# Attention, routed MoE and gated MLP on one core: a second expert item taken before all tokens are routed

## Chip, cores, metric
One NeuronCore of a Trainium2 chip runs the kernel. The metric is device time of one execution in microseconds (us), the median of the runs shown. All inputs come from the reference's own setup with seed 0.

## The reference, cut to what matters
```python
# attention: B=8, H=8, S=576, D=64; k and v are averaged over 8 neighbours (72 keys)
k_p = k.reshape(B, H, 72, 8, D).mean(axis=3); v_p = v.reshape(B, H, 72, 8, D).mean(axis=3)
attn = softmax(q @ k_p^T / sqrt(D)); x = (attn @ v_p) as (4608, 512)

# mixture of experts: 8 experts, one for each token; 512 -> 1024 -> 512
e_idx = argmax(x @ w_gate, axis=1)
gate_w = softmax(x @ w_gate)[e_idx]; eom = sigmoid(x @ w_output_gate)
for e in range(8):
    mask = e_idx == e
    out[mask] = gate_w[mask] * eom[mask, e] * (relu(x[mask] @ w1[e]) @ w2[e])

# gated MLP: 512 -> 2048 -> 512
h = out @ w_in; y = (h * sigmoid(h)) @ w_out
```

## The kernel before
The order of the instructions on every engine is written out by hand (`tc.manual_schedule()`): each engine works off its own queue in the order in which the Python code emits, and waits at an instruction whose operands aren't there.

**Attention.** The 4608 tokens are 36 tiles of 128. The loop over `u` (L790) runs two half-steps for each tile, u = 2 to 74; step u turns probabilities (`turn_p`, tile `psp`), multiplies by the values (`values`, tile `pv`, three steps late) and computes scores two or three steps ahead. After a tile's values follow its normalised rows (`r`, `xg` on VectorE), written to the DRAM table `xd`, and its gate logits (`gh`, `gl`).

**Routing.** Tiles are routed in groups (`GROUPS`). When the last tile of a group is in, `gate_ops` gives 21 small operations: the token's expert, its place in the expert's list by the `rank` matmuls, its weight. They go to a background queue from which `bg` takes 2 or 4 a step. Then each tile of the group is scattered by one GpSimd indirect DMA (`scatter`, L585, with six small memsets ahead of it, L584) into the table `idd`: one slot of (token, weight) for each token, sorted by expert. `SCAT` says how many steps after the group's end the scatters start, and how many go in two steps.

**The early item.** After group `EARLY` (24 tiles) `early_ops` picks the expert with most tokens so far. GpSimd gathers the ids and weights of its first 3 x 128 tokens from `idd` (`e_gid`, L652, in step `EG`), TensorE turns them (`e_ps`, L661, in step `ET`), and GpSimd gathers the tokens' rows from `xd` (`e_x`, L636, in step `EX`). These three blocks are the first item of the next stage, which can so begin before all tokens are routed.

**Expert items.** The MoE stage is a row of items, each with three, two or one block of 128 tokens of one expert (A, C and S in `ORDER`). Item 0 is the early one. An item of two or three blocks has 8 units; unit u is `l2(u)` (9 matmuls `y`, L1219, for three blocks) behind `l1(u+1)` (12 matmuls `h`, L1173). Weights come as four pairs of 512 KB loads on SyncE's queue (`load_w`, L1096 and L1099), after SyncE has read the expert's number (L1092), and are split into high and low parts on ScalarE and VectorE. Rows of an item are gathered by `gather_x` (L1121), turned by `trans_x` (`trx`, L1143) and split. Items of at most the fixed numbers of `ORDER` run always; what the counted tokens need beyond them runs behind a branch.

**What `pre` puts into item 0.** The dict `pre` holds what follows `l2(u)` of a unit: the last group's gate operations in -1 and 0, then its four scatters; the eight scatters of the group before (`kept_scat`) at the stage's start; the plan of the other items (`route`, 28 small VectorE operations) in units 1 and 2; the gather of all items' ids (`gather_ids`, tile `gid`, L891); in unit `GSTEP` = 5 `turn_ids`, which turns the ids on TensorE (`psi`, L1047) into `idx`, and the gather of item 1's rows. From unit 6 on the MLP's weights are decoded beside the items.

Finished items are scattered to the DRAM table `yd` (the early one is written to `ye`), from which the MLP stage reads its blocks (`yin`).

Of the kernel before, what the change touches and what calls it, by code (L numbers as in the profile page):

```python
# [8 lines left out]
F32 = mybir.dt.float32  # L9
# [19 lines left out]
GROUPS = (8, 12, 4, 8, 4)  # L29
# [10 lines left out]
SLOTS = ((NBLK - 3 + E - 1) // 3, 2 * E, E)  # L40
EARLY = 3
PACE = 6
REST = N - 3 * P
# [5 lines left out]
GSTEP = 5  # L49
# [36 lines left out]
STARTV = ((26, 2), (44, 3))  # L86
ORDER = "ACACASACACASACA"
# [31 lines left out]
def kernel(  # L119
# [30 lines left out]
    ye = tc.dram_tile([3 * P, DM], F32, name="ye")  # L150
# [479 lines left out]
    e_idx = const.tile([P, 1], I32, tag="e_idx", name="e_idx")  # L630
    e_ids = const.tile([P, 3], I32, tag="e_ids", name="e_ids")
    e_w = const.tile([P, 3], F32, tag="e_w", name="e_w")
    e_x = [lp.tile([P, DM], F32, tag=f"e_x{i}", name=f"e_x{i}") for i in range(3)]

    def early_x(i):
        nc.gpsimd.indirect_dma_start(  # L636
            out=e_x[i],
            out_offset=None,
            in_=xd[0 : G0[EARLY] * P, :],
            in_offset=bass.IndirectOffsetOnAxis(ap=e_ids[:, i : i + 1], axis=0),  # L640
        )

    def early_ops():
        def tl(shape, tag, dt=F32):
            return lp.tile(shape, dt, tag=f"e_{tag}", name=f"e_{tag}")

        n = tl([P, E], "n")
        mx, cand, best, row = tl([P, 1], "mx"), tl([P, E], "cand"), tl([P, 1], "best"), tl([P, 1], "row", I32)
        gid, gif = tl([3, P, 2], "gid", I32), tl([3, P], "gif")
# [9 lines left out]
        def turn():  # L659
            ps = bank("e_ps", "pr")  # L660
# [23 lines left out]
            lambda: nc.vector.tensor_tensor(out=row, in0=cand[:, 0:1], in1=pcol, op=ALU.add),  # L684
            lambda: nc.vector.scalar_tensor_tensor(
                out=e_off, in0=e_hot, scalar=-3.0 * P, in1=ebase, op0=ALU.mult, op1=ALU.subtract
            ),
        ], gather, lambda: nc.vector.tensor_copy(out=gif, in_=gid[:, :, 0]), turn
# [102 lines left out]
    kept_scat = []  # L791
    UN = 2 * NT
    for u in range(2, UN + PVL):
# [22 lines left out]
        if odd and 0 <= t < NT:  # L816
            gates(t)
            if t + 1 in G0:
                g = G0.index(t + 1) - 1
                ops, scat = gate_ops(g, gp if g < NG - 2 else lp, rank_ps)  # L820
                (at(GAT[g], bgq.extend, ops) if g in GAT else bgq.extend(ops))
                for i, f in enumerate(scat):
                    step = u + SCAT[g][0] + 2 * i // SCAT[g][1]
                    if step < UN + PVL:
                        at(step, f)
                    else:
                        kept_scat.append(f)
                if g + 1 == EARLY:
                    ops, ga, tu, tv = early_ops()
                    bgq.extend(ops)  # L830
                    at(EG, ga)
                    at(ET, tu)
                    item.append((ET, tv))
                    for i in range(3):
                        at(EX, early_x, i)
# [805 lines left out]
```

## Time and profile before
| | us |
|---|---|
| median of 3 runs | 1490.28 |
| the runs | 1485.74, 1490.87, 1490.28 |
| the profiled execution | 1488.13 |
| its span in the trace | 1486.4 |

| engine | busy, us | share of the span |
|---|---|---|
| TensorE (PE) | 1422.4 | 96% |
| VectorE (DVE) | 934.0 | 63% |
| ScalarE (ACT) | 652.5 | 44% |
| GpSimd (POOL) | 395.5 | 27% |

A busy share is the time in which an engine had an instruction in work. The profile also gives the clock that TensorE was granted in a stretch, as a fraction of 2.4 GHz: 1.00 is the upper of its two levels, 0.50 the lower (1.2 GHz). The span mean is 0.987. A timeline row gives the start of an instruction (or of several merged ones), its length, engine, line, operation, the tile written <- the tiles read, and in brackets the engine's idle time before it with what ended that. Attention runs to about 197 us, the expert items to about 700 us, the MLP to the end.

### The profile page before, as it was taken

Reading aid. Unit: us, or ns where it says so; the run is one execution under the profiler, and the core shown is the slowest. Engines: PE = TensorE matmul, PEld = TensorE weight load, DVE = VectorE, ACT = ScalarE, POOL = GpSimd, SP = SyncE. Lnnn points to the kernel's source line nnn. Section 1 sums busy time; section 2 is a strip of 40 time slices with the busy share of each in tenths; the row PEclk is TensorE's granted clock in tenths of the full one; section 3 lists DMA queues with packets and bytes.
Section 4 is the critical chain, followed back from the end, with each engine's and each line's share of the span. In section 5 each row is a group of like instructions: output and inputs, shape, how many; then the busy total and the mean of one; then the engine's idle time right before and its main releaser. Section 6 shows DMA issues by size and latency. Waiting matters only on the chain.

```text
span 1486.4 us, 22198 instructions
## 1 busy us (share of the span) xinstructions
PE 1422.4 (96%) x7923; PEld 1262.0 (85%) x7924; DVE 934.0 (63%) x1709; ACT 652.5 (44%) x1312; POOL 395.5 (27%) x629
## 2 busy tenths in 40 slices
PE   8999895999999999999999999999999999999996
PEld 6989784898989988898888888888888988988885
DVE  5677682889879778874753555645555565465443
ACT  4767542555566555662332423433343243234222
POOL 1766662446445334531020200120030012001001
PEclk9999997999999999999999999999999999999998
DMA  9999166688787766884989566567458557645441
GB/s 263 264 228 193 54 171 179 205 284 286 253 306 280 251 218 234 302 232 124 336 276 284 177 162 186 162 180 184 147 178 172 182 159 194 179 139 191 159 135 43
DMA packets 259370, 302.88 MB, mean 204 GB/s; under 512 B 157849, under 2 KB 190620, under 8 KB 250419
## 3 DMA queue, kind: packets, MB, share of 16 engines
q1 hardware_dynamic: 247042, 271.06, 62.4%
q0 software_dynamic: 11776, 29.53, 5.5%
q8 instruction: 64, 1.05, 0.3%
q10 hardware_dynamic: 432, 0.79, 0.1%
q14 instruction: 56, 0.45, 0.1%
HBM read 251.70 MB, written 50.41 MB: 203 GB/s over the span
## 4 chain that ended last, share of the span: by engine, by line
PE 41%; DVE 4%; ACT 4%; another core or an unknown queue 1%; issue 1%; DMA 1%; SPq 1%; POOL 0%; ACTq 0%; POOLq 0%; DVEq 0%
PE o L1455 22%; PE b L1411 8%; PE a L1411 6%; DVE sg L1429 1%; ACT gh L1432 1%; ACT t L1009 1%; SPq L985 1%; ACT os L1465 1%; DMA wQ<-wid 1%; DVE gl L1437 1%; DVE b L1010 0%; ACT sg L1425 0%; DVE t L1010 0%; DMA yin<-yd 0%
## 5 line engine op out<-in xcount | busy, mean ns | idle before, releaser
L1455 PE MATMUL o<-woh,gh 128*128 128x512 f32 x576 | 228.2, 396 | 1.3 <-ACT gh L1432 1.1
L1455 PE MATMUL o<-wol,gh 128*128 128x512 f32 x576 | 228.8, 397 | 0.0
L1455 PE MATMUL o<-woh,gl 128*128 128x512 f32 x576 | 228.0, 396 | 0.0
L1467 POOL DMA_INDIRECT out_dram<-os,ids x33 | 35.7, 1083 | 623.3 <-ACT os L1465 619.4
L1432 ACT CAST gh<-sg 128x384 fp32r<-128x384 f32 x192 | 98.6, 513 | 146.3 <-DVE sg L1429 145.1
L1437 DVE TENSOR_TENSOR gl<-sg,gh 128x384 fp32r<-128x384 f32 x192 | 107.3, 559 | 75.4 <-ACT gh L1432 64.6
L1455 PEld LDWEIGHTS o<-woh,gl 128*128 128x128 f32 x576 | 108.1, 188 | 28.9 <-DVE gl L1437 3.4
L1455 PEld LDWEIGHTS o<-woh,gh 128*128 128x128 f32 x576 | 108.1, 188 | 22.2 <-ACT gh L1432 4.5
L1455 PEld LDWEIGHTS o<-wol,gh 128*128 128x128 f32 x576 | 108.1, 188 | 17.3
L1425 ACT ACTIVATE sg<-a 128x384 f32<-128x384 f32 x56 | 27.5, 491 | 165.5 <-PE a L1411 157.9
L1411 PE MATMUL a<-b,wA 128*128 128x384 f32 x480 | 98.0, 339 | 2.0 <-ACT t L1572 2.0
L1411 PE MATMUL b<-t,wS 128*128 128x384 f32 x480 | 97.2, 336 | 0.2
L1411 PEld LDWEIGHTS a<-b,wA 128*128 128x128 f32 x480 | 85.6, 188 | 6.9 <-ACT t L1572 3.3
L1411 PEld LDWEIGHTS b<-t,wS 128*128 128x128 f32 x480 | 85.2, 188 | 5.6 <-DVE u L1420 1.8
L503 PE MATMUL pv<-vb,pT 72*128 72x128 f32 (+1 forms) x640 | 80.7, 277 | 0.3 <-DVE gh L537 0.3
L1420 DVE TENSOR_TENSOR u<-b,t 128x384 f32<-128x384 f32 x40 | 22.3, 557 | 89.1 <-PE b L1411 86.5
L503 PEld LDWEIGHTS pv<-vb,pT 72*128 72x128 f32 (+1 forms) x640 | 73.6, 182 | 2.0 <-issue 1.2
L482 ACT ACTIVATE pe<-sc,nm 128x72 f32<-128x72 f32 x288 | 67.7, 319 | 11.9 <-DVE nm L476 11.6
L1425 ACT ACTIVATE sg<-t 128x384 f32<-128x384 f32 x40 | 21.0, 525 | 108.9 <-DVE t L1420 102.7
L1429 DVE TENSOR_TENSOR sg<-a,sg 128x384 f32<-128x384 f32 x56 | 31.1, 555 | 48.6 <-ACT sg L1425 45.3
L492 ACT COPY pT<-psp 72x512 f32<-72x512 f32 x72 | 41.8, 581 | 40.3 <-PE psp L488 36.3
L476 DVE TENSOR_REDUCE nm<-sc 128x4 f32<-128x288 f32 x72 | 32.4, 452 | 29.9 <-PE sc L466 19.0
(3780 smaller groups left out, 3589.0 us busy)
## 6 DMA issues: line engine op xcount, KB each, us to landing
wS<-wis SPq DMA_DIRECT2D x40, 1024.0 KB
wA<-wid SPq DMA_DIRECT2D x40, 768.0 KB
wol<-wold SPq DMA_DIRECT2D x112, 256.0 KB
wQ<-wid SPq DMA_DIRECT2D x16, 1024.0 KB
yin<-yd SPq DMA_DIRECT2D x44, 192.0 KB
xd<-xg SPq DMA_DIRECT2D x32, 256.0 KB
raw_i<-in_moe_w_in_dram SPq DMA_DIRECT2D x16, 512.0 KB
wid<-em SPq DMA_DIRECT2D x8, 1024.0 KB
```

Source lines behind the costliest of these rows:

```text
L476: nc.vector.tensor_reduce(out=nm_t[u], in_=sc_t[u], op=ALU.max, axis=AX.X, negate=True)
L482: nc.scalar.activation(out=pe[:, h * NK : h * NK + NK], in_=ps[:, h, :], func=AF.Exp, bias=nm[:, h, :])
L492: nc.scalar.copy(out=pT_t[u], in_=ps_t.pop(u))
L503: nc.tensor.matmul(pv_t[t][o : o + n, j % 2, VW * c : VW * c + VW], pT[:, j, o : o + n], vw[b][:, HG * h : HG * h + VW], start=True, stop= ...
L1411: nc.tensor.matmul(ps, w[:, o, i, c, :], x[:, c, :], start=(first and k == 0), stop=(k == 5), skip_group_check=True)
L1420: nc.vector.tensor_tensor(out=o, in0=a, in1=b, op=ALU.add)
L1425: nc.scalar.activation(out=g_t[key][0], in_=h, func=AF.Sigmoid)
L1429: nc.vector.tensor_tensor(out=sg, in0=h, in1=sg, op=ALU.mult)
L1432: nc.scalar.copy(out=gh, in_=sg)
L1437: nc.vector.tensor_tensor(out=gl, in0=sg, in1=gh.bitcast(F32), op=ALU.subtract)
L1455: nc.tensor.matmul(o_t[sb, a][s], x[:, sl_], w, start=(k0 == 0 and k == 0), stop=(k0 == 2 * NFP - 1 and k == 2))
L1467: ins = nc.gpsimd.indirect_dma_start(out=out, out_offset=bass.IndirectOffsetOnAxis(ap=(id_t[b][:, s, 0:1] if b else e_ids[:, s : s + 1]), ...
```

## The change
A second early item is taken after 28 tiles, besides the one after 24. `early_ops(k)` runs twice; the second pick takes the expert with most tokens left (the first pick's 384 are off its count) and, if it is the same expert, the next three blocks (`both`). Item 1 is now that second early item: its ids are turned by a second `e_ps` behind unit 0, and its rows gathered right there through `e_ids[1]`. The first planned item is item 2, whose rows follow `turn_ids` in unit `GSTEP` = 9 where item 1's followed in unit 5. `ORDER` loses one A; the other 14 items stay in their order, so there are 16 items and 39 blocks before and after. The groups are 12, 8, 4, 4, 8 tiles; all of the first four are scattered within attention (`kept_scat` is gone), and the last group, now 8 tiles, has its gate operations and its scatters in units 1 and 2. `ye` holds six blocks and `yd` three fewer.

```diff
-GROUPS = (8, 12, 4, 8, 4)
+GROUPS = (12, 8, 4, 4, 8)
-SLOTS = ((NBLK - 3 + E - 1) // 3, 2 * E, E)
-EARLY = 3
+EARLY = (3, 4)
+NE = len(EARLY)
+SLOTS = ((NBLK - 3 * NE + E - 1) // 3, 2 * E, E)
-GSTEP = 5
+GSTEP = 9
-EG = 63
-ET = 66
-EX = 68
-GAT = {0: 27}
-SCAT = ((13, 2), (11, 3), (9, 2), (10, 2))
+EG = (61, 72)
+ET = 69
+EX = 71
+SCAT = ((12, 2), (6, 3), (6, 4), (6, 4))
-STARTV = ((26, 2), (44, 3))
-ORDER = "ACACASACACASACA"
+STARTV = ((26, 2), (40, 3))
+ORDER = "CACASACACASACA"
...
+        else:
+            ops += [
+                lambda: nc.vector.tensor_tensor(out=n, in0=hot, in1=e_hot, op=ALU.mult),
+                lambda: nc.vector.tensor_reduce(out=both, in_=n, op=ALU.add, axis=AX.X),
+                lambda: nc.vector.tensor_tensor(out=best, in0=cand[:, 0:1], in1=pcol, op=ALU.add),
+                lambda: nc.vector.scalar_tensor_tensor(
+                    out=row, in0=both, scalar=3.0, in1=best, op0=ALU.mult, op1=ALU.add
+                ),
...
-        bg(4 if u >= 52 or GAT[0] <= u < GAT[0] + 6 else 2)
+        bg(4 if u >= 44 or 28 <= u < 34 else 2)
...
             def rows(j, i):
+                if items[j][1] < 0:
+                    return e_ids[-1 - items[j][1]][:, i : i + 1]
                 c = col(j, i)
...
-                    src = e_idx[0:1, :] if items[j][1] < 0 else eji[p : p + 1, :]
+                    src = e_idx[-1 - items[j][1]][0:1, :] if items[j][1] < 0 else eji[p : p + 1, :]
...
-                    nc.scalar.dma_start(out=ye[i * P : (i + 1) * P, :], in_=ys)
+                    nc.scalar.dma_start(out=ye[j * TB + i * P : j * TB + (i + 1) * P, :], in_=ys)
...
-                if fc == (7 if pre and j == 0 else 3 if one else GU):
+                if not early and fc == (3 if one else GU):
...
+        def turn_late():
+            turn_e[0]()
+            turn_e[1](pby.tile([P, 512], F32, tag="y", name="e_ps"))()
+
         pre = {
-            -2: kept_scat,
-            -1: gate[:turn],
-            0: gate[turn + 1 :] + scat,
-            1: route[:14],
-            2: route[14:] + [gather_ids],
-            GSTEP: [turn_ids, "gather"],
+            0: [turn_late, 1],
+            1: gate[:turn],
+            2: gate[turn + 1 :] + scat,
+            4: route[:14],
+            5: route[14:],
+            6: [gather_ids],
+            GSTEP: [turn_ids, 2],
...
-            pre[7 + i // 3] = ranks[i : i + 3]
-        pre[13] = [turn_ranks]
+            pre[10 + i // 3] = ranks[i : i + 3]
+        pre[14] = [turn_ranks]
```

TensorE at the end of unit 5, before (`y` is l2, `h` is l1; `psi` turns the gathered ids, `xt` are item 1's rows):

```order
L1219 MATMUL y_0_-1_0_3274<-hi_0_-1_2_3379,hl_-1_5_3489 128x512
L1047 MATMUL psi<-ident,rkf 128x79
L1048 MATMUL psi<-ident,gid 128x79
L1143 MATMUL trx_-1_1_3545<-ident,xt_0_-1_1_3537 128x128 x4
L1173 MATMUL h_-1_7_3560<-xh_-1_0_3194,hi_0_-1_3_3424 128x384
```

TensorE at the end of unit 9, the second unit of item 1, in the changed kernel:

```order
L1243 MATMUL y_0_-1_1_3709<-hi_0_-1_4_3577,hh_-1_9_3694 128x512
L1243 MATMUL y_0_-1_1_3709<-lo_0_-1_4_3578,hh_-1_9_3694 128x512
L1243 MATMUL y_0_-1_1_3709<-hi_0_-1_4_3577,hl_-1_9_3695 128x512
L1069 MATMUL psi<-ident,rkf 128x76
L1070 MATMUL psi<-ident,gid 128x76
L1197 MATMUL h_-1_11_3788<-xh_-1_1_3568,hi_0_-1_5_3635 128x384
```

The two turns of the gathered ids stood behind 6 units of matmuls and right ahead of a turn of the rows fetched by them; now they stand behind 10 units, and two units of matmuls follow before the first rows fetched by them are turned.

TensorE near the end of attention, before (`e_ps` turns the ids of the early item):

```order
L466 MATMUL sc_1_2785<-kbd_116,qT_2659 128x144 x2
L661 MATMUL e_ps<-ident,e_gif 128x3
L662 MATMUL e_ps<-ident,e_gid 128x3
L488 MATMUL psp_2797<-ident,pe_2740 72x128 x4
L503 MATMUL pv_2811<-vb_1879,pT_2711 128x128 x4
L466 MATMUL sc_0_2816<-kbd_116,qT_2728 128x144 x2
```

The same place in the changed kernel, followed to the first turn of item 0's rows:

```order
L489 MATMUL psp_2936<-ident,pe_2884 72x128 x4
L504 MATMUL pv_2950<-vb_1706,pT_2835 128x128 x4
L667 MATMUL e_ps<-ident,e_gif_2646 128x3
L668 MATMUL e_ps<-ident,e_gid_2645 128x3
L489 MATMUL psp_2965<-ident,pe_2915 72x128 x4
L504 MATMUL pv_2950<-vb_1706,pT_2882 128x128 x4
L489 MATMUL psp_2983<-ident,pe_2945 72x128 x4
L504 MATMUL pv_2990<-vb_1706,pT_2913 128x128 x4
L504 MATMUL pv_2990<-vb_1706,pT_2943 128x128 x4
```

The turn has moved three steps towards the end: two `psp` steps and their values now stand behind it, where there were five.

GpSimd from the scatters of the last group to the gathers of the first planned items, before (`sli_4` are that group's slots, `xt` item 1's rows, `e_x` item 2's):

```order
L585 DMA idd<-idw,sli_4_3110 37888x2
L891 DMA gid<-idd,rowi 79x256
L1121 DMA xt_0_-1_1_3537<-xd,idx 128x512
L1121 DMA xt_0_-1_1_3539<-xd,idx 128x512
L1121 DMA xt_0_-1_1_3541<-xd,idx 128x512
L1121 DMA e_x_152<-xd,idx 128x512
L1121 DMA e_x_153<-xd,idx 128x512
```

GpSimd in the changed kernel, from the same scatters (`mh_i` and `em` belong to the decode of the MLP's weights, `e_x` are item 2's rows):

```order
L586 DMA idd<-idw,sli_4_3156 37888x2
L913 DMA gid<-idd,rowi 76x256
L252 TENSOR_TENSOR mh_i_0_3665<-mh_i_0_3665,em_0_3670 128x512
L272 TENSOR_TENSOR em_0_3670<-mh_i_0_3665,e_i_0_3623 128x4x128
L1145 DMA e_x_155<-xd,idx 128x512
L1145 DMA e_x_156<-xd,idx 128x512
```

Item 1's three gathers no longer stand behind `gid`, and a pair of decode operations stands between `gid` and item 2's gathers.

## Rows read from the trace of the kernel before

**Rows 1.** The page: busy time of each engine, and TensorE in 40 slices.

```profile
PE 1422.4 (96%) x7923; PEld 1262.0 (85%) x7924; DVE 934.0 (63%) x1709; ACT 652.5 (44%) x1312; POOL 395.5 (27%) x629
PE   8999895999999999999999999999999999999996
```

**Rows 2.** Stretches: length, busy of PE, PEld, DVE, ACT, POOL, clock, DMA share, GB/s.

```profile
180.00:186.00 6.00, 2.04 (x11) 1.93 (x12) 2.21 (x10) 1.53 (x6) 2.71 (x9) 0.61 0.01 2
240.00:250.00 10.00, 1.43 (x7) 1.22 (x8) 0.47 (x2) 0.22 (x1) 3.52 (x4) 0.50 0.26 74
270.00:300.00 30.00, 28.10 (x150) 24.52 (x149) 26.29 (x44) 14.80 (x23) 13.75 (x10) 1.00 0.75 245
```

**Rows 3.** Timeline of PE, end of attention.

```profile
169.03 0.60 PE L488 MATMUL psp<-ident,pe 128*72 128x128 f32 x4
...
170.85 0.60 PE L488 MATMUL psp<-ident,pe 128*72 128x128 f32 x4
...
183.96 0.26 PE L661 MATMUL e_ps<-ident,e_gif 3*128 3x3 f32 x1 [5.86 <-DVE e_gif L688]
...
184.26 1.07 PE L488 MATMUL psp<-ident,pe 128*72 128x128 f32 x4
...
187.79 0.76 PE L488 MATMUL psp<-ident,pe 128*72 128x128 f32 x4
...
196.89 0.60 PE L1143 MATMUL trx_-1_0_3196<-ident,e_x 128*128 128x128 f32 x4
...
201.88 0.66 PE L1173 MATMUL h_-1_0_3226<-xh_-1_0_3194,hi_-1_0_3190 128*128 128x384 f32 x1 [3.52 <-issue]
```

**Rows 4.** Timeline of POOL, end of attention and item 0.

```profile
175.16 0.97 POOL L585 DMA_INDIRECT idd<-idw,sli  x1 [0.16 <-issue]
...
177.10 0.96 POOL L585 DMA_INDIRECT idd<-idw,sli  x1 [0.16 <-issue]
181.47 0.92 POOL L652 DMA_INDIRECT e_gid<-idd,e_row  x1 [3.41 <-issue]
...
188.31 0.95 POOL L636 DMA_INDIRECT e_x<-xd,e_ids  x1 [0.30 <-issue]
...
233.82 1.93 POOL L891 DMA_INDIRECT gid<-idd,rowi  x1 [9.07 <-DMA r_-1_5_3472<-in_moe_w_dram]
245.56 0.99 POOL L1121 DMA_INDIRECT xt_-1_1_3537<-xd,idx  x1 [9.81 <-DVE idx L1049]
```

**Rows 5.** Timeline of DVE, end of attention and item 0.

```profile
196.66 0.16 DVE L617 TENSOR_SCALAR e<-ex 128x8 f32<-128x8 f32 x1
...
201.70 0.68 DVE L1146 TENSOR_TENSOR xl_-1_0_3195<-trx_-1_0_3210,xh_-1_0_3194 128x512 fp32r<-128x512 f32 x1
...
211.96 0.18 DVE L623 RECIPROCAL idw<-sm 128x4 f32<-128x4 f32 x1
...
244.19 0.23 DVE L1045 CAST rkf<-gid 79x128 f32<-79x128 int32 x1 [13.84 <-DMA gid<-idd,rowi]
```

**Rows 6.** Timeline of PE, items 0 and 1.

```profile
209.87 0.26 PE L569 MATMUL rank<-ohb,tri 128*128 128x8 bf16 x4
...
244.48 0.39 PE L1047 MATMUL psi<-ident,rkf 79*128 79x79 f32 x1 [13.21 <-DVE rkf L1045]
...
249.09 1.09 PE L1143 MATMUL trx_-1_1_3545<-ident,xt_-1_1_3537 128*128 128x128 f32 x4 [4.09 <-DMA xt_-1_1_3537<-xd,idx]
249.84 0.67 PE L1173 MATMUL h_-1_7_3560<-xh_-1_0_3194,hi_-1_3_3424 128*128 128x384 f32 x1
...
253.09 0.33 PE L1173 MATMUL h_-1_7_3560<-xl_-1_0_3195,hi_-1_3_3424 128*128 128x384 f32 x1
...
266.77 0.33 PE L1173 MATMUL h_-1_10_3713<-xh_-1_1_3543,hi_-1_5_3609 128*128 128x384 f32 x1
...
270.95 0.33 PE L1173 MATMUL h_-1_11_3765<-xh_-1_1_3543,hi_-1_5_3609 128*128 128x384 f32 x1
```

**Rows 7.** SyncE's queue, 190 to 275 us: waiter, cause, total us, times, longest.

```profile
SPq L1092 <- DVE eji L933: 16.7, 1, 16.7
```

More of the change, by code (lines that the diff above doesn't have):

```diff
@@ L629 @@
     e_off = const.tile([P, E], F32, tag="e_off", name="e_off")
-    e_idx = const.tile([P, 1], I32, tag="e_idx", name="e_idx")
-    e_ids = const.tile([P, 3], I32, tag="e_ids", name="e_ids")
-    e_w = const.tile([P, 3], F32, tag="e_w", name="e_w")
+    e_idx, e_ids, e_w = (
+        [const.tile([P, w], dt, tag=f"{nm}{k}", name=f"{nm}{k}") for k in range(NE)]
+        for nm, w, dt in (("e_idx", 1, I32), ("e_ids", 3, I32), ("e_w", 3, F32))
+    )
     e_x = [lp.tile([P, DM], F32, tag=f"e_x{i}", name=f"e_x{i}") for i in range(3)]
@@ L638, in early_x, with early_ops @@
             out_offset=None,
[L639 to L640 removed]
+            in_=xd[0 : G0[EARLY[0]] * P, :],
+            in_offset=bass.IndirectOffsetOnAxis(ap=e_ids[0][:, i : i + 1], axis=0),
         )
[L643 removed]
+    def early_ops(k):
         def tl(shape, tag, dt=F32):
[L645 to L647 removed]
+            return lp.tile(shape, dt, tag=f"e_{tag}", name=f"e_{tag}{k}")
+        n, hot, both = tl([P, E], "n"), e_hot if k == 0 else tl([P, E], "hot"), k and tl([P, 1], "both")
         mx, cand, best, row = tl([P, 1], "mx"), tl([P, E], "cand"), tl([P, 1], "best"), tl([P, 1], "row", I32)
[L649 removed]
+        own = {}
         def gather():
+            own[0] = lp.tile([3, P, 2], I32, tag="e_gid", name=f"e_gid{k}")
+            own[1] = lp.tile([3, P], F32, tag="e_gif", name=f"e_gif{k}")
+            gid = own[0]
             nc.gpsimd.indirect_dma_start(
@@ L657, in gather, with turn @@
             )
-        def turn():
-            ps = bank("e_ps", "pr")
+        def turn(ps):
+            gid, gif = own[0], own[1]
             nc.tensor.transpose(ps[:, 0:3], gif, ident[0:3, 0:3])
@@ L683, in early_ops @@
             ),
[L684 to L688, printed above, removed]
+        ]
+        if k == 0:
+            ops += [
+                lambda: nc.vector.tensor_tensor(out=row, in0=cand[:, 0:1], in1=pcol, op=ALU.add),
+                lambda: nc.vector.scalar_tensor_tensor(
+                    out=e_off, in0=e_hot, scalar=-3.0 * P, in1=ebase, op0=ALU.mult, op1=ALU.subtract
+                ),
+            ]
+        else:
+            ops += [
+                lambda: nc.vector.tensor_tensor(out=n, in0=hot, in1=e_hot, op=ALU.mult),
+                lambda: nc.vector.tensor_reduce(out=both, in_=n, op=ALU.add, axis=AX.X),
+                lambda: nc.vector.tensor_tensor(out=best, in0=cand[:, 0:1], in1=pcol, op=ALU.add),
+                lambda: nc.vector.scalar_tensor_tensor(
+                    out=row, in0=both, scalar=3.0, in1=best, op0=ALU.mult, op1=ALU.add
+                ),
+                lambda: nc.vector.scalar_tensor_tensor(
+                    out=e_off, in0=hot, scalar=-3.0 * P, in1=e_off, op0=ALU.mult, op1=ALU.add
+                ),
+                lambda: nc.vector.tensor_tensor(out=e_hot, in0=e_hot, in1=hot, op=ALU.add),
+            ]
+        return ops, gather, lambda: nc.vector.tensor_copy(out=own[1], in_=own[0][:, :, 0]), turn
     load_kv(0, 0, ((0, 3), (3, 6), (6, N9)))
@@ L819 @@
                 g = G0.index(t + 1) - 1
-                ops, scat = gate_ops(g, gp if g < NG - 2 else lp, rank_ps)
-                (at(GAT[g], bgq.extend, ops) if g in GAT else bgq.extend(ops))
+                ops, scat = gate_ops(g, gp, rank_ps)
+                bgq.extend(ops)
                 for i, f in enumerate(scat):
[L823 to L829, printed above, removed]
-                    bgq.extend(ops)
[L831 to L835, printed above, removed]
+                    at(u + SCAT[g][0] + 2 * i // SCAT[g][1], f)
+                if g + 1 in EARLY:
+                    k = EARLY.index(g + 1)
+                    ops, ga, *turn_e = early_ops(k)
+                    bgq.extend(ops)
+                    at(EG[k], ga)
+                    if k == 0:
+                        at(ET, turn_e[0])
+                        item.append((ET, lambda tv=turn_e[1]: evac.append(tv(bank("e_ps", "pr")))))
+                        for i in range(3):
+                            at(EX, early_x, i)
         if u % 2 == 0 and QD <= u // 2 + QA < NT:
             emit_qT(u // 2 + QA)
-        bg(4 if u >= 52 or GAT[0] <= u < GAT[0] + 6 else 2)
+        bg(4 if u >= 44 or 28 <= u < 34 else 2)
     assert not item, item
@@ L1116, in gather_x @@
                     return
-                if items[j][1] < 0:
+                if items[j][1] == -1:
                     xg_t[j, i] = e_x[i]
@@ L1320 @@
         todo_ = dict.fromkeys(NAMES, 0)
-        items = [(0, -1)]
+        items = [(0, -1 - k) for k in range(NE)]
         for ch in ORDER:
```

37 lines of the change are left out of this document (18 added, 19 removed).

## The prediction
> **What bounds the kernel now.** I read the page first: TensorE is busy 1422.4 of 1486.4 us, and no other engine over 63% [rows 1]. So time can be won only where TensorE stands still, or runs at its lower clock. In its 40 slices nearly every digit is 9; the early dips are in the slices that hold 180 and 240 us, the seam between attention and the experts [rows 1]. The windows put numbers on them: from 180 to 186 TensorE works 2.04 of 6 us at a clock of 0.61, from 240 to 250 it works 1.43 of 10 us at 0.50 [rows 2]. The timelines name the waits. Two are long.
>
> First stall: before `e_ps` TensorE stands 5.86 us, for the ids of the early item [rows 3]. Their gather left GpSimd at 181.47, after 3.41 us behind its last scatter [rows 4]: the scatters have to land first. So GpSimd's row of scatters sets this end.
>
> Second stall: before `psi` it stands 13.21 us and before item 1's first turn 4.09 us more [rows 6]. Here the ids' gather waited 9.07 us on GpSimd, again behind scatters [rows 4]; the profile names a weight load there, but the load is no input of the gather, and what it reads is the scattered table. Its landing took another 10.4 us, from 233.82 to the cast's start at 244.19 [rows 4, 5]. The cast itself stood 13.84 us at the head of VectorE's queue, so the high and low parts queued behind it were late too.
>
> **The first stall (A).** What it costs: 5.86 us idle, and then a slow stretch. A step of attention takes 1.82 us at full clock (169.03 to 170.85) and took 3.53 right after the stall (184.26 to 187.79), 1.71 more [rows 3]. Together 7.6 us. The change puts the gather at step 61 for 63 and the turn at 69 for 66, and moves the scatters. A scatter with its six memsets takes 1.95 us of GpSimd (175.16 to 177.10) [rows 4]. The last twelve that the gather needs are now due from six steps after their groups' ends, the first from step 50 (tile 19's logits are done in step 44), 13 steps of 1.82 before 169.03, which is step 63: 145; 12 x 1.95 is 23.4, so the last leaves by 169, where it left at 177.10. Behind it the 3.41 us, then a landing of 2.2 us (from 181.47 to 183.7, where the turn's wait ended, less the cast's 0.2) or, by the other gather, 10.4: in by 175 to 183. The turn is due three steps after where TensorE stopped (183.96 - 5.86 = 178.1), at 183.5. Even the slow end is in time, so the stall goes. VectorE is relieved at this place too: an operation of a group's routing ran there as late as 196.66 [rows 5], amid the last rows of attention; now the group that is routed inside attention last is the one of 28 tiles, and its 21 operations are done before. With item 0's splits close behind (to 201.70) I take 0.5 us, so 8.1.
>
> Next late is item 0's rows. Before, their third gather was issued at 188.31, 4.35 us after `e_ps` [rows 3, 4], with 8.6 us to the first turn. So now the third gather goes at about 187.9, and its rows are wanted for VectorE's third split, 8.1 us earlier than 201.70, behind a turn and a copy of 0.6 each: at 192.4. Landing takes between 3.5 us (the rows of item 1: issued 245.56, ended the wait at 249.09, DMA share 0.26 there) and 10.4 (the ids above) [rows 2, 4, 6]. That is 191.4 or 198.3: no loss, or 5.9. The item's weight loads leave SyncE at about the same time, so neither row fits; I take 5.5 us, nearer to the quiet row since the gathers are few, which is 1.0 late. **A = 7.1 us**, between 2.2 and 8.1.
>
> The Trainium skill, "DMA: Bandwidth & Descriptors", section "Queues, rings and completion order", says that each DMA engine takes turns, a packet at a time, between the queue rows that have work. By that a gather on GpSimd's queue is not held until the weights on SyncE's queue have drained; A would be 8.1 and the whole time 1 us lower. The 10.4 us row speaks against it, for in this trace a gather of a few KB did take that long beside weight loads.
>
> **The second stall (B).** Its whole price: 13.21 + 4.09 us idle; ten products of unit 7's l1 from 249.84 to 253.09 in 3.25 us, at a clock of 0.50 [rows 2], so half of it, 1.6, is the clock's; the turn at 1.09 where 0.60 is usual, so 0.5 [rows 3, 6]. **19.4 us.** It goes if the ids are in when TensorE comes to `psi`. Count from the start of `l1(0)`, T (201.88 before). A unit takes 4.18 us (266.77 to 270.95) [rows 6]. Before, the last group's ranks came at T + 8.0 [rows 6]; now they follow l2(2), two units later, T + 16.4. From the rank to the last gate operation VectorE took 2.3 us (209.87 to 211.96 and 0.18) [rows 5, 6]; for 8 tiles I take 3: first scatter at T + 19.5. Eight scatters take 15.6: T + 35. The wait behind the last scatter was 3.41 us in quiet and 9.07 under load, the landing 2.2 or 10.4 [rows 3 to 5]. So the ids are in between T + 41 and T + 54. `psi` is due after unit 9 at about T + 48. Slack between +7 and -6. I choose no stall, because the load of before had a reason that is gone: SyncE had waited 16.7 us for the route's expert number [rows 7] and sent its held loads in a burst just as scatters and ids were under way. Item 1's number now comes from the early pick, so its loads go out as buffers come free. The same wait now stands before item 2's loads, 8 units later, with the route in units 4 and 5 far ahead of it.
>
> **What the new order adds.**
> - Item 2's rows. They leave after `idx`, 1.1 us behind `psi` (244.48 to 245.56) [rows 4, 6], and are turned two units, 8.4 us, behind it; 3.5 us of landing fit, 10.4 are 3.1 late, and GpSimd has two decode operations ahead of them. The stretch there is loaded (DMA share 0.75) [rows 2]. I take 0.8, from 0 to 5.
> - The second `e_ps` on TensorE is 0.26 and its pair: 0.3 [rows 3]. Its gather leaves GpSimd right after item 0's, at about 189, and is wanted at T + 6.2, about 200; even 10.4 us of landing fit.
> - The twelve rank operations move from units 7 to 10 into 10 to 13, next to item 2's turns, on a VectorE that is busy 26.29 of 30 us there [rows 2]. I take 0.6, from 0 to 2.5.
> - 13 more VectorE operations of the second pick, at about 0.2 us each (the reciprocal took 0.18) [rows 5], lie in attention beside TensorE's work; uncovered they would cost 2.7, I take 0. `xd`'s rows for items 0 and 1, three more writes to `ye` on ScalarE's queue and three fewer scatters on GpSimd's, the fewer rows of `yd`: nothing waits on them; 0.
> - Attention's own groups: 12 tiles first, then 8. The operations are wider and earlier; the number of them is the same. 0, by a step's worth either way: -0.7 to +0.7.
> - The number of items and blocks is the same, 16 and 39, since on these inputs the second pick finds six blocks (722 tokens by tile 28) and the plan then needs 7, 5 and 2 items, as `ORDER` has them.
>
> **The sum.** 7.1 + 19.4 - 0.8 - 0.3 - 0.6 = 24.8 us. From the profiled 1488.13 that is 1463.3; it ran 2.15 under the median of the three runs (1490.28), and from that it would be 1465.5. I take **1464** (1460 to 1468 with the terms' small ends).
>
> **Rivals.**
> 1. The ids come late a second time, at `psi` after unit 9. For it: the 9.07 and 10.4 us rows [rows 4, 5], eight scatters instead of four, and the same single queue. Against: the burst is gone. All loaded, 6 us idle; an idle of 5.86 also cost 1.7 of clock [rows 3]. It would take back up to 7.7, I price 6: **1470**. It decides when ids land later than T + 48.
> 2. Rows come late: item 0's at the full 10.4 (4.9 more than in the sum), or item 2's (2.3 more). For: item 0's gathers go out beside 3 MB of weights. Against: the quiet row. **1468**.
> 3. The change moves the stall whole: whatever holds the ids lasts longer than the four units gained, as if each later scatter also landed later. B comes back, 24.8 - 19.4: **1482 to 1485**, which is no change by the bound below. Against: four units are 16.7 us, as long as the stall.
> 4. Slower. The plan needs more A items than the seven in `ORDER`. A pick from an expert with only four blocks leaves eight A items, and the eighth runs behind the branch after the sixteenth: 8 units of 4.18 us, 33.4, and a start of its own, as from 188.31 (rows asked for) to 201.88 (first product), 13.6 [rows 3, 4, 6]. 47 less 24.8 is 22 slower: **1510**. It decides at 512 tokens of the picked expert; the reference's inputs give 722, so only a pick that goes astray brings it.
>
> **Chances and range.** Forecast 0.63, rival 1 0.16, rival 2 0.15, rival 3 0.03, rival 4 0.03. The range goes down to 1459 (quiet rows in every term, and attention 0.7 better) and up to 1473 (rival 1 at its full price); it leaves out rivals 3 and 4 and thin tails. A measurement of this kernel can tell 0.5%, about 7.5 us, from no change. Faster by more: 0.94; within: 0.03; slower: 0.03.
>
> **What would show it.** In the new trace: no idle before `e_ps` and a clock of 1.00 from 180 on (A); less than 2 us before the first `trx` and the first `h` of item 0; item 1's first turn without a wait; `psi` after unit 9 without one (B), with the ids' cast no longer waiting at VectorE's head; no wait of SyncE for `eji` at item 1; little before item 2's first turn. I am wrong if GpSimd's gather of the ids still waits 9 us and lands in 10 without a burst beside it, if item 0's rows hold TensorE for over 3 us, or if the sum holds and the end comes later: then VectorE from 270 on is what I missed.

## The result

The changed kernel took 1470.38, 1472.66, 1476.10 and 1472.57 us, median 1472.62, beside a fourth run of the kernel before that makes its median 1489.10. The ratio is 0.9894, with a 95% interval of 0.9867 to 0.9921: about 16 us faster, where I had forecast 26. The direction was right; some 10 us are missing. 0.9894 of the 1490.28 that I started from is 1474.5, beyond the upper end of my range; the median itself, 1472.62, lies just inside it.

The profiled execution (1470.38 us, span 1468.7) against that of before (span 1486.4), at four places of TensorE's timeline:

| place | before | after | difference | the sum said |
|---|---|---|---|---|
| last turn of probabilities | 192.87 | 189.44 | -3.4 | about -8 |
| first turn of item 0's rows | 196.89 | 198.13 | +1.2 | -7 |
| first turn of item 2's rows | 279.35 | 263.17 | -16.2 | -25 |
| end of the span | 1486.4 | 1468.7 | -17.7 | -25 |

From the second place to the third the change won 17.4 us, as the terms B and its costs said (17.7). What is missing was lost ahead of it, twice. A part of the first loss is hidden in the table: when step 30 of attention began (88.24, and 93.89 before), the changed run was already 5.7 us ahead, and 2.7 of these were there at the second turn of probabilities (16.73 for 19.42), where the two kernels still do the same. That start differs from trace to trace, 16.66 to 19.42 in all of this case, so 2.7 us of the -17.7 are chance. The profile after:

```profile
PE 1423.2 (97%) x7926; PEld 1267.8 (86%) x7926; DVE 943.3 (64%) x1725; ACT 653.4 (44%) x1312; POOL 390.2 (27%) x618
PE   8999989999999999998999999999999999999996
PEclk9989989999999999999999999999999999999998
```

The dips of [rows 1] at 180 and 240 us are gone, but the clock's line has new ones, in the slice from 73 to 110 us and in the one from 184 to 220, where TensorE's own line dips too. Windows (columns as in [rows 2]):

```profile
96.00:100.00 4.00, 2.01 (x11) 1.54 (x10) 3.90 (x12) 2.41 (x10) 0.83 (x1) 0.79 1.06 232
100.00:104.00 4.00, 4.00 (x23) 3.75 (x22) 3.25 (x13) 1.57 (x6) 0.03 (x1) 0.50 1.03 386
...
180.00:186.00 6.00, 6.00 (x56) 5.61 (x55) 4.91 (x24) 3.60 (x13) 4.27 (x18) 1.00 0.25 90
...
198.00:210.00 12.00, 11.11 (x40) 9.42 (x41) 5.51 (x7) 5.76 (x9) 2.39 (x4) 0.60 0.79 292
...
240.00:250.00 10.00, 9.71 (x49) 8.63 (x49) 7.30 (x10) 4.78 (x8) 4.54 (x3) 1.00 0.46 115
```

180 to 186 and 240 to 250, the two stalls of before, now run at full clock with a busy TensorE. From 100 to 104, inside attention, TensorE is fully busy at half its clock; from 198 to 210, in item 0, nearly so. **First loss**, the timelines of TensorE, VectorE and GpSimd there:

```profile
94.38 0.66 PE L467 MATMUL sc<-kbd,qT 128*128 128x144 f32 x4
...
98.35 1.33 PE L467 MATMUL sc<-kbd,qT 128*128 128x144 f32 x4 [1.99 <-DVE xg L524]
...
103.45 1.17 PE L467 MATMUL sc<-kbd,qT 128*128 128x144 f32 x4
```
```profile
87.06 2.10 DVE L555 TENSOR_TENSOR ohb<-cand,best 128x96 bf16<-128x96 f32 x1
...
92.25 1.93 DVE L555 TENSOR_TENSOR oh<-cand,best 128x96 f32<-128x96 f32 x1
...
94.11 0.25 DVE L555 TENSOR_TENSOR ex<-gl,mx 128x96 f32<-128x96 f32 x1
...
94.28 2.67 DVE L555 TENSOR_TENSOR sel<-oh,gl 128x96 f32<-128x96 f32 x1
```
```profile
86.15 5.22 POOL L362 TENSOR_TENSOR kv<-kv 128x1280 f32<-128x1280 f32 x2 [4.04 <-DMA kv<-in_k_dram]
91.45 2.62 POOL L366 TENSOR_TENSOR kv<-kv 128x1152 f32<-128x1152 f32 x1
94.15 2.68 POOL L368 TENSOR_TENSOR ks<-kv 128x1152 f32<-128x1152 f32 x1
```

Three routing operations of the first group take 2 to 2.7 us where their like takes 0.25, and each of the last two ends within 0.13 us of a GpSimd addition: `oh` at 94.18 (91.45 + 2.62 = 94.07), `sel` at 96.95 (94.15 + 2.68 = 96.83). The rows `xg` queue behind them, the scores wait 1.99 us, and the clock falls to 0.50. By the steps of attention, seven of them took 28.4 us (88.24 to 116.65) where they took 16.9 before: 11.5 us, of which only 2 are that wait. Before, the first scatter stood ahead of the additions in GpSimd's queue and held them until the group was routed:

```profile
102.19 1.14 POOL L585 DMA_INDIRECT idd<-idw,sli  x1 [13.88 <-DVE idw L623]
103.37 5.22 POOL L361 TENSOR_TENSOR kv<-kv 128x1280 f32<-128x1280 f32 x2
```

The Trainium skill, "SBUF — State Buffer", section "SBUF: two separate sides", says that VectorE and GpSimd share one pair of ports as an exclusive lock: an operation with two SBUF inputs and a GpSimd operation that reads SBUF do not overlap; the later one waits the whole of the other. The two end times agree with it to 0.13 us.

**Second loss**, at item 0's start (TensorE, then GpSimd):

```profile
187.81 0.22 PE L667 MATMUL e_ps<-ident,e_gif 3*128 3x3 f32 x1
...
198.13 1.11 PE L1167 MATMUL trx_-1_0_3186<-ident,e_x 128*128 128x128 f32 x4 [4.49 <-DMA e_x<-xd,e_ids]
199.20 1.12 PE L1167 MATMUL trx_-1_0_3193<-ident,e_x 128*128 128x128 f32 x4
...
202.16 0.69 PE L1197 MATMUL h_-1_0_3211<-xh_-1_0_3184,hi_-1_0_3180 128*128 128x384 f32 x1 [0.68 <-ACT xh_-1_0_3184 L1169]
```
```profile
188.61 1.00 POOL L639 DMA_INDIRECT e_x<-xd,e_ids  x1 [1.03 <-DVE gh L538]
```

No wait stands before `e_ps` any more (5.86 in [rows 3]). But the first rows, asked for at 188.61, landed at 198.13, 9.5 us later; TensorE waited 4.49 us, and behind that ran at half its clock: the turns take 1.1 us for 0.6, the twelve products of `l1(0)` 4.4 us for 2.1. That is some 4.8 us more than at full clock. The kernel before had a wait and a low clock at this place too, behind the turns: 3.52 us before the first product [rows 3], and `l1(0)` in 3.8 us. Against it the loss is 4.3 us: from the last turn of probabilities to the first product of `l1(1)` it took 12.8 us (192.87 to 205.70), the changed kernel 17.1 (189.44 to 206.57).

### The profile page after: what moved, and what is told of

It is laid out like the page before. It is cut to its first block, busy times and chain, and to the rows that moved or that the text cites. A ratio compares the mean times of both kernels' runs of the same rounds, so it can differ in the third digit from the quotient of the medians.

```text
span 1468.7 us, 22211 instructions
## 1 busy us (share of the span) xinstructions
PE 1423.2 (97%) x7926; PEld 1267.8 (86%) x7926; DVE 943.3 (64%) x1725; ACT 653.4 (44%) x1312; POOL 390.2 (27%) x618
## 4 chain that ended last, share of the span: by engine, by line
PE 41%; DVE 5%; ACT 4%; issue 1%; SPq 1%; DMA 0%; POOL 0%; another core or an unknown queue 0%; ACTq 0%; DVEq 0%; POOLq 0%
PE o L1485 21%; PE b L1441 8%; PE a L1441 6%; DVE sg L1459 1%; ACT gh L1462 1%; ACT t L1031 1%; DVE gl L1467 1%; ACT sg L1455 1%; DVE W L1547 1%; ACT os L1495 1%; ACT ems L1557 1%; SPq L1007 1%; DVE b L1032 0%; DVE t L1032 0%; DMA yin<-yd 0%
## 5 line engine op out<-in xcount | busy, mean ns | idle before, releaser
L1497 POOL DMA_INDIRECT out_dram<-os,ids x30 | 32.1, 1071 | 561.4 <-ACT os L1495 558.0
L467 PE MATMUL sc<-kbd,qT 128*128 128x144 f32 (+1 forms) x320 | 50.7, 301 | 2.3 <-DVE xg L524 2.0
```

What stands on the lines that cost most here:

```text
L467: nc.tensor.matmul(ps[o : o + n, 2 * c : 2 * c + 2, :], qT_t[t][:, 2 * hf + c, o : o + n], kbds[b // 2 % 2][:, h0 : h0 + 5 : 4, :], start= ...
L1497: ins = nc.gpsimd.indirect_dma_start(out=out, out_offset=bass.IndirectOffsetOnAxis(ap=(id_t[b][:, s, 0:1] if b >= NE else e_ids[b][:, s : ...
```

## The experiments

Four questions: is the first loss that collision; what would win back the second; was the first stall of before really set by GpSimd's row of scatters; and was it the four units of lead that removed the second stall? Times are medians; the ratio is to the kernel before, run beside.

**x2_before_pool_free**: the collision put into the kernel before.

```diff
-SCAT = ((13, 2), (11, 3), (9, 2), (10, 2))
+SCAT = ((15, 2), (11, 3), (9, 2), (10, 2))
```

> The kernel before, with the scatters of its first group two steps later (step 35 instead of 33), so that GpSimd's pooling additions of the last k (step 34) stand ahead of the first scatter in its queue and needn't wait until that group is routed. Theory 1: the kernel before was spared the collision only by this order; now the additions start as soon as k is in, about 86 us, beside the group's operations: some of these take 1.5 to 2.7 us, TensorE waits and may lose its clock: slower by 3 to 12 us, 1492 to 1501. Rival (the width of the group is to blame): 8 tiles as before, no change, 1488 to 1491.

1490.58 us, ratio 1.0025 [1.0010, 1.0041]: slower by 0.25%, less than I expected, and scattered: ten runs from 1487.2 to 1497.2. The median alone lies in the rival's range; what decides is the trace. The profiled one is among the slow (1496.68) and shows the thing itself, with a group of 8 tiles (VectorE, then TensorE):

```profile
98.56 2.46 DVE L554 TENSOR_TENSOR pos<-pos,oh 128x64 f32<-128x64 f32 x1
...
101.30 2.34 DVE L615 CAST sli<-sl 128x8 int32<-128x8 f32 x1
```
```profile
104.21 1.34 PE L429 MATMUL vw<-wg,vbt 64*72 64x80 f32 x8 [3.05 <-DVE vb L432]
```

Its steps 33 to 37 lose 11.1 us. Why only some runs lose it was not tried. When the additions start hangs on when k lands (5.48 us of waiting for that DMA ahead of them here), and x12, below, shows such a wait without the low clock behind it.

**x1_group0_late**: the operations moved, the additions left.

```diff
-                bgq.extend(ops)
+                (at(33, bgq.extend, ops) if g == 0 else bgq.extend(ops))
...
-        bg(4 if u >= 44 or 28 <= u < 34 else 2)
+        bg(4 if u >= 44 or 33 <= u < 39 else 2)
```

> The changed kernel, with the routing operations of the first group (12 tiles) put into VectorE's queue at step 33 instead of 28. Theory 1: in the changed kernel these operations run beside GpSimd's pooling additions of k, each waits until a GpSimd addition ends (2.10, 1.93 and 2.67 us where 0.26 is usual), TensorE's scores then wait 1.99 us, and the clock falls to 0.50 for five steps; late by five steps, they miss the additions: no operation of that group over 0.5 us, clock 1.00 from 84 to 120, and about 10 us off 1472.6: 1461 to 1465. Rival: a group of 12 is simply more work at one place than VectorE has room for: the wait of TensorE and the low clock come at a later step, 1470 to 1474.

1466.83 us (1463.75 to 1474.68), ratio 0.9881 [0.9847, 0.9914]. Neither: the operations miss the additions of k and hit those of v, which start at 103.89:

```profile
104.92 1.99 DVE L555 TENSOR_TENSOR oh<-cand,best 128x96 f32<-128x96 f32 x1
106.83 2.39 DVE L555 TENSOR_TENSOR ex<-gl,mx 128x96 f32<-128x96 f32 x1
```

**x5_pool_held**: the additions held behind the first scatter, as the kernel before had them.

```diff
-SCAT = ((12, 2), (6, 3), (6, 4), (6, 4))
+SCAT = ((6, 2), (6, 3), (6, 4), (6, 4))
-... (34, 3, 0), (34, 3, 1))
+... (35, 3, 0), (35, 3, 1))
```

> The changed kernel, with the first group's scatters from step 34 instead of 40 and GpSimd's pooling additions of the last k and v in step 35 instead of 34, so that, as in the kernel before, the first scatter stands ahead of the additions in GpSimd's queue and holds them until the group is routed. Theory 1: no operation of the group over 0.5 us, no wait of TensorE and clock 1.00 from 84 to 124; about 10 us off the changed kernel, 1460 to 1464. Rival 1 (width of the group): the stall and the low clock stay, 1470 to 1474. Rival 2: the additions, now some 10 us later, are missed by the turns of k (step 41), and TensorE waits there instead: 1466 to 1472.

1467.61 us, ratio 0.9871 [0.9855, 0.9888]. Attention does what theory 1 says: no operation of the 12-tile group over 0.26 us, full clock, and the last turn of probabilities at 180.40, 9.0 us ahead of the changed kernel. So the width is not to blame. But only 3 to 5 of the 9 us reach the end (by the ratios and by the medians), since the rows come little sooner (GpSimd, then TensorE):

```profile
183.09 1.00 POOL L639 DMA_INDIRECT e_x<-xd,e_ids  x1 [0.30 <-DVE r L517]
...
191.06 1.11 PE L1167 MATMUL trx_-1_0_3186<-ident,e_x 128*128 128x128 f32 x4 [6.46 <-DMA e_x<-xd,e_ids]
```

**x3_rows_early**: the rows asked for earlier.

```diff
-SCAT = ((12, 2), (6, 3), (6, 4), (6, 4))
+SCAT = ((12, 2), (6, 3), (6, 4), (8, 4))
-ET = 69
-EX = 71
+ET = 66
+EX = 68
-            0: [turn_late, 1],
...
-            2: gate[turn + 1 :] + scat,
+            2: [turn_late, 1] + gate[turn + 1 :] + scat,
```

> The changed kernel, with the first item's ids turned in step 66 instead of 69, its rows gathered in step 68 and ahead of the fourth group's scatters (which start two steps later), and the second item's ids turned behind unit 2 instead of 0. Theory 2: in the changed kernel the first item's rows, asked for at 188.6 among six weight loads, land at 198.1 and cost 4.49 us of waiting and 4.8 us of low clock behind it (products of l1(0) at 0.32 us for 0.17); asked for some 6 us earlier they are in time: no wait before the first turn, clock 1.00 from 186 to 210, 7 to 9 us faster, 1463 to 1466. Rival: the weights themselves are as late as the rows, and TensorE waits for their split at the first product instead: 1470 to 1473.

1467.59 us (1460.30 to 1470.29), ratio 0.9852 [0.9818, 0.9885]: 5 to 6 us under the changed kernel, between the two. The wait for rows is gone and the turns run at full clock; a wait for the split of the weights has taken part of its place:

```profile
195.30 0.60 PE L1167 MATMUL trx_-1_0_3186<-ident,e_x 128*128 128x128 f32 x4
...
199.67 0.45 PE L1197 MATMUL h_-1_0_3211<-xh_-1_0_3184,hi_-1_0_3180 128*128 128x384 f32 x1 [2.89 <-ACT hi_-1_0_3207 L1133]
```

**x6_held_and_rows_early**: x5 and x3 together, here against x5.

```diff
-SCAT = ((6, 2), (6, 3), (6, 4), (6, 4))
-ET = 69
-EX = 71
+SCAT = ((6, 2), (6, 3), (6, 4), (9, 4))
+ET = 67
+EX = 69
-            0: [turn_late, 1],
...
-            2: gate[turn + 1 :] + scat,
+            2: [turn_late, 1] + gate[turn + 1 :] + scat,
```

> The kernel x5_pool_held, and beside it the first item's ids turned in step 67 and its rows gathered in step 69, ahead of the fourth group's scatters, and the second item's ids turned behind unit 2. Theories 1 and 2 together: attention without its low clock (10 us) and no wait for rows before the first turn; what remains there is the wait of about 3 us for the first weights' split, as in x3_rows_early: 1453 to 1459. Rival: with attention 10 us earlier the weights, whose loads wait for attention's buffers, or the ids become late by as much, and the gain of the two doesn't add: 1460 to 1466.

**1459.25 us** (1456.04 to 1461.69), ratio 0.9815 [0.9797, 0.9833]: 12 to 13 us under the changed kernel, where each part alone gave 3 to 6. This version beats both kernels. What is left of waiting before item 0's first product is small, though the products of `l1(0)` still run at half clock (4.1 us for 2.1):

```profile
186.79 0.65 PE L1167 MATMUL trx_-1_0_3200<-ident,e_x 128*128 128x128 f32 x4 [0.61 <-DMA e_x<-xd,e_ids]
...
188.97 0.41 PE L1197 MATMUL h_-1_0_3211<-xh_-1_0_3184,hi_-1_0_3180 128*128 128x384 f32 x1 [1.53 <-DVE xl_-1_0_3185 L1170]
```

**x11_weights_held**: does the weight burst make the rows slow? x5, with four of the six loads behind the rows.

```diff
             for n in range(3):
+                if pre and n == 1:
+                    nc.sync.dma_start(out=held, in_=e_x[2][0:1, 0:16])
                 load_w(n)
```

> The kernel x5_pool_held, with one small write on SyncE's queue that reads the last of the first item's gathered rows, placed between the first item's first and second pair of weight loads: four of the six 512 KB loads now leave only when the rows are in. In x5_pool_held the rows were asked for at 183.1 and landed at 191.1, 8.0 us, while all six loads were in flight, and TensorE waited 6.46 us. Theory 2 (the rows share the transfer engines with the weight burst): they land after 4 to 5 us, the wait falls below 4 us: 1463 to 1466. Rival: 8 us is what such a gather takes at this place whatever runs beside it; the wait stays within 1 us of 6.5, and later loads make it 1468 to 1472.

1465.59 us, ratio 0.9854 [0.9838, 0.9871]. The rows took 6.4 us (183.53 to 189.97) for 8.0, the wait 5.03 for 6.46; the time can't be told from that of x5.

```profile
183.53 1.00 POOL L640 DMA_INDIRECT e_x<-xd,e_ids  x1 [0.30 <-issue]
...
189.97 1.11 PE L1168 MATMUL trx_-1_0_3188<-ident,e_x 128*128 128x128 f32 x4 [5.03 <-DMA e_x<-xd,e_ids]
```

Five traces with all six loads beside the rows (the changed kernel, x1, x5, x9, x12) show 8.0 to 9.5 us, so the burst makes at least 1.6 us, and the greater part stays though four of the six loads are held. What makes the rest is open. One rival was left untested: in all six of these traces the four scatters of the fourth group stand right ahead of the rows in GpSimd's queue. In x3 the rows go ahead of them, and the quickest of its gathers landed 3.7 us after its issue (185.45 to 189.15); but there the loads too were issued only from 188.12 on. **x13_all_held**, the same hold in x6:

> The kernel x6_held_and_rows_early with the same hold of four weight loads behind the first item's rows as in x11_weights_held. If rows and weights only exchange their places in the transfers, the rows' waits of 0.36 and 0.61 us go and the first weights are split earlier (1.53 us before the first product), but the third pair comes later: 1457 to 1460, no difference to 1459.25 that can be told. Rival: the held loads are late for unit 2 and TensorE stands there: 1462 to 1466.

1461.12 us (1456.95 to 1469.51), ratio 0.9831 [0.9793, 0.9870]: no difference that can be told. The rows' two waits are gone, and the wait before the first product grew from 1.53 to 2.89 us.

**x10_before_scatter_early** and **x7_before_turn_late**: the first stall, in the kernel before. x10:

```diff
-SCAT = ((13, 2), (11, 3), (9, 2), (10, 2))
+SCAT = ((13, 2), (6, 3), (6, 2), (10, 2))
-        bg(4 if u >= 52 or GAT[0] <= u < GAT[0] + 6 else 2)
+        bg(4 if u >= 44 or GAT[0] <= u < GAT[0] + 6 else 2)
```

> The kernel before, with the second and third groups' scatters due six steps after their groups' ends (11 and 9 before, the third four in two steps as its two), and four instead of two routing operations a step from step 44. My prediction's reading of the first stall: GpSimd's row of scatters sets it. The last scatter the ids need then ends some 6 to 9 us earlier, the 5.86 us wait and the low clock behind it go, and nothing else is moved: 1480 to 1483. Rival: the ids' landing lengthens as in x7_before_turn_late, since the weight loads move up too, and at least 4 of the 5.86 us stay: 1485 to 1489.

1479.54 us, ratio 0.9949 [0.9930, 0.9968]. x7:

```diff
-ET = 66
-EX = 68
+ET = 69
+EX = 71
```

> The kernel before, with only the early item's ids turned in step 69 instead of 66 and its rows gathered in step 71 instead of 68. My prediction's term A, the turn alone: the wait of 5.86 us before it is gone and most of 7 us is won, 1481 to 1484. Theory 2: the rows now leave about 5.5 us later than they did, among the weight loads, land after 9 to 10 us, and the wait with its low clock stands before the first turn of the item instead: 1486 to 1492.

1487.81 us, ratio 1.0007 [0.9997, 1.0018]. `e_ps` in x10 and in x7, and in x7 its ids' gather and their cast:

```profile
178.24 0.22 PE L661 MATMUL e_ps<-ident,e_gif 3*128 3x3 f32 x1 [0.34 <-DVE e_gif L688]
```
```profile
188.48 0.26 PE L661 MATMUL e_ps<-ident,e_gif 3*128 3x3 f32 x1 [5.74 <-DVE e_gif L688]
```
```profile
182.73 0.92 POOL L652 DMA_INDIRECT e_gid<-idd,e_row  x1 [5.00 <-DVE best L557]
```
```profile
188.21 0.21 DVE L688 CAST e_gif<-e_gid 3x128 f32<-3x128 int32 x1 [6.43 <-DMA e_gid<-idd,e_row]
```

Scatters 6 us earlier end the stall, and all of the 7.6 us arrive (0.51% of 1487.41; 4.8 to 10.4 by the interval). A turn three steps later ends nothing, and not for the reason that theory 2 gave: the ids left 1.3 us later than before and took 5.5 us where they took 2.2, with the first item's weight loads, issued from 180.9 (188.0 before), now beside them. The lead was eaten by the later start and the longer landing.

**x12_turn_at_7**: the second stall, in the changed kernel.

```diff
-GSTEP = 9
+GSTEP = 7
```

> The changed kernel with the turn of the planned items' ids in unit 7 instead of 9. My prediction's term B says that the second stall goes because TensorE has four more units of work before that turn, while the ids themselves come no sooner. Then the turn, 8.4 us earlier, waits 1.4 + 8.4 = about 10 us, the clock falls behind it, and the whole is 9 to 12 us slower than the changed kernel: 1481 to 1485. Rival (spreading the routing, or the absence of the burst, made the ids come sooner than the turn and something else sets the 1.41 us): the wait stays under 4 us, 1472 to 1476.

1473.52 us, ratio 0.9908 [0.9891, 0.9924], not slower than the changed kernel by anything that can be told. But the profiled run hides the price: attention ended 7.0 us earlier in it (last turn of probabilities at 182.44), and from there to the end of the span it took 1284.1 us where the changed kernel took 1279.3, so 4.8 more. Attention was quicker although the collision stands in this trace too. TensorE waits as long as in the changed kernel, but then keeps a clock of 1.00, and steps 30 to 36 take 20.6 us for 28.4 (28.8 and 28.1 in x3 and x9). Why the clock fell in three of these four traces and not here stays open:

```profile
99.30 0.76 PE L467 MATMUL sc<-kbd,qT 128*128 128x144 f32 x4 [2.13 <-DVE xg L524]
```
```profile
100.00:104.00 4.00, 4.00 (x39) 3.69 (x39) 3.79 (x15) 2.64 (x10) 0.47 (x1) 1.00 0.98 312
```

The wait before the turn is back, 4.0 us for the 10 that I expected. GpSimd, VectorE and TensorE in x12:

```profile
236.25 1.16 POOL L913 DMA_INDIRECT gid<-idd,rowi  x1 [6.83 <-DMA idd<-idw,sli]
```
```profile
239.69 0.22 DVE L1067 CAST rkf<-gid 76x128 f32<-76x128 int32 x1 [4.55 <-DMA gid<-idd,rowi]
```
```profile
240.06 0.36 PE L1069 MATMUL psi<-ident,rkf 76*128 76x76 f32 x1 [4.01 <-DVE rkf L1067]
```

The ids are in 45.6 us after `l1(0)` starts (194.11 to 239.69), 3.4 us after their gather left. That is the quick end: no weight load leaves SyncE from 228.3 to 243.1 us in this trace. In the changed kernel three leave beside the gather (246.00, 247.45, 249.45), and it landed 6.3 us after 245.35, at 251.6, which is 49.5 us after `l1(0)` starts. Its gather, the landing as the trace gives it for the tile `gid`, and the turn:

```profile
245.35 1.65 POOL L913 DMA_INDIRECT gid<-idd,rowi  x1 [7.42 <-DVE sg_i L232]
```
```profile
DMA to landing us min/median/max: 6.3/6.3/6.3
```
```profile
254.56 0.26 PE L1069 MATMUL psi<-ident,rkf 76*128 76x76 f32 x1 [1.41 <-DVE rkf L1067]
```

TensorE was free for the turn at 253.15, so the ids came 1.5 us ahead of it. The 1.41 us before `psi` were no wait for ids, though its releaser is the cast of them:

```profile
252.59 1.23 DVE L1135 TENSOR_TENSOR lo_-1_6_3728<-r_-1_6_3581,hi_-1_6_3727 128x1024 fp32r<-128x1024 f32 x1 [1.39 <-ACT hi_-1_6_3727 L1133]
253.73 0.55 DVE L1202 SCALAR_TENSOR_TENSOR hl_-1_10_3745<-h_-1_10_3731,hh_-1_10_3744 128x384 fp32r<-128x384 f32 x1
254.20 0.21 DVE L1067 CAST rkf<-gid 76x128 f32<-76x128 int32 x1
```

The cast stands in VectorE's queue behind other work and ran without an idle gap; it says when VectorE got there, not when the ids came. A spare of 1.5 us is little. In x3, x6 and x13, which turn item 1's ids two units later, the ids do come late; the cast stands idle for them, and TensorE waits 2.64, 1.46 and 3.50 us before `psi` (the casts of x3, x6 and x13):

```profile
251.76 0.22 DVE L1067 CAST rkf<-gid 76x128 f32<-76x128 int32 x1 [1.10 <-DMA gid<-idd,rowi]
```
```profile
240.03 0.22 DVE L1067 CAST rkf<-gid 76x128 f32<-76x128 int32 x1 [0.28 <-DMA gid<-idd,rowi]
```
```profile
244.24 0.23 DVE L1068 CAST rkf<-gid 76x128 f32<-76x128 int32 x1 [1.95 <-DMA gid<-idd,rowi]
```

**x9_decode_late**: made on the wrong reading that the ids took 9 us to land (6.3, as said above) and that TensorE waited for them.

```diff
-            if n_b(j) == 1 or u < 6 or u >= PREP - 1:
+            if n_b(j) == 1 or u < 12 or u >= PREP - 1:
```

> The changed kernel, with the decode of the MLP's weights started at unit 12 instead of 6, so that none of its 512 KB loads run while the last scatters and the ids' gather are under way. The ids' gather there waited 7.42 us behind its last scatter and landed after 9.1 us, and TensorE waited 1.41 us for it. Theory: these are the price of the decode's loads beside it: the wait falls to 4 us and the landing below 5, TensorE doesn't wait at unit 9, 1470 to 1472. Rival: the weight loads of the items alone are enough to hold it: both stay within 1.5 us of what they were, and TensorE waits 1 to 2 us.

1484.79 us, ratio 0.9975 [0.9958, 0.9993]. The wait behind the last scatter stayed (8.03 us), so the decode's loads are not its cause; TensorE waited 0.45 us before `psi`. And with the decode pressed into fewer units TensorE is busy 188.4 of the 200 us from 300 to 500, where it was busy 198.9, which is most of the 12 us that this run lost on the changed kernel.

## Why the prediction was half right

The two stalls were read rightly and both went. Two terms ahead of them failed: "Attention's own groups", put at 0, cost 11.5 us, and item 0's rows, put at 1.0 us late, held TensorE for 4.49 us.

- **A, the wait before `e_ps`: right.** Its cause was the row of scatters, its price 7.6 us; x10 took it away in the kernel before and won 7.6. But x7 shows that the later turn, which my sum also counted on, would not have done it.
- **Item 0's rows: mis-sized.** I took 5.5 us of landing between 3.5 and 10.4, and 1.0 late; the first rows took 9.5, and the wait was 4.49. The step that failed is the choice of the value: "nearer to the quiet row since the gathers are few". With the loads beside them x5 shows 8.0, with fewer loads x11 6.4: there was no quiet at this place to be near to. And I left out what such a wait costs behind itself, although I had priced it for `e_ps`: 4.8 us of low clock, 9.3 with the wait. So rival 2, at 4.9, was the right mechanism. Against the kernel before the place cost 4.3 us net, since that had a wait and a low clock of its own there. My own sign of being wrong, rows that hold TensorE for over 3 us, came true.
- What I worked out from the Trainium skill, "DMA: Bandwidth & Descriptors", section "Queues, rings and completion order", a landing as quick as the quiet row, did not come. That the engines take turns between queues may still hold: with four of the six loads held, x11's rows landed 1.6 us sooner, so rows and loads do bear on each other.
- **Attention's groups, "0, -0.7 to +0.7": wrong, and the largest miss.** It cost 11.5 us in the profiled run, and 3.7 in x12, where the clock held (20.6 for the 16.9 us of before). I counted operations and widths, and did not ask what GpSimd does at that time. Before, the first scatter (step 33) stood ahead of the pooling (step 34) in GpSimd's queue and held it until the group was routed; with the scatter in step 40 the pooling ran beside the routing. x2 and x5 make and unmake that with one or two numbers.
- **B: right in size, its margin partly luck.** 17.4 us against 17.7. Item 0 itself adds almost nothing to this: from its first turn to its first product `y` it takes 10.9 us before and 11.0 after, since the wait before its first product is 2.8 us shorter (3.52 to 0.68) and the low clock costs that much more, neither of which I had counted. No wait for ids is left, as chosen, but by 1.5 us only: they came at T + 49.5, and TensorE was free at T + 51.0, where I had set T + 48. In x3, x6 and x13 it went the other way by 1 to 3 us, a small form of rival 1. The four units of lead are needed: with two fewer, in x12, the wait is back although the ids came at T + 45.6. The rows of before were not as far off as "the burst is gone" made them: the gather still waited 7.42 us behind the last scatter and landed in 6.3. How much the burst had made was not tried.
- **The costs.** Item 2's first turn had no wait (0.8 in the sum), the second `e_ps` none; in item 2 a product `y` waits 0.9 us for VectorE, in unit 17. I had set 0.6 for the ranks in units 10 to 13; whether the two belong together was not looked into.
- Rivals 3 and 4 did not happen, and in the changed kernel rival 1 did not.

The terms do not add because each stall hides the next: with attention repaired (x5) the rows' wait grows from 4.49 to 6.46, with the rows repaired (x3) attention's loss still stands. Only both together (x6) give 28 us against the kernel before (1487.41 to 1459.25), the size of the forecast.

## What to carry to other kernels

Moving a step in a queue also frees what stood behind it: ask what then starts earlier, on which engine, and beside what. Price a wait of TensorE with the low clock that may follow: here 2.0 us cost 11.5 and 4.5 cost 9.3, but 2.1 us at the same place in x12 cost 3.7, with the clock at 1.00. So a single trace of such a stretch is not its price. A releaser that stands in an engine's own queue gives the time at which that engine came to it; only an idle gap ended by the transfer, or the trace's own landing time, tells when the data came.

## What was not expected of the hardware

An operation on VectorE beside an addition on GpSimd took up to 2.67 us for 0.25, and ended with it; a reduction from one input (`gl` 0.37) and operations that read PSUM (`nm` 0.45, `xg` 0.69) in the same stretch kept their time. In x2 a cast with a single input was held too (2.34 us for 0.17). The first of three gathers of 128 rows took 8.0 to 9.5 us with six 512 KB loads issued around it, and 6.4 with two. The clock fell to 0.50 behind a wait of 1.99 us in the changed kernel and stayed at 1.00 behind one of 2.13 us at the same place in x12.
